# Two-bank score tiles for the first two batches of an attention and mixer kernel

## The chip, the cores and the metric

The kernel runs on one core of one Trainium2 chip. The time is that of the device for one launch, in microseconds, and the median of several runs is compared. A core has four engines that compute, each with an instruction queue of its own that runs in order: TensorE (PE, with its weight loads shown as PEld), VectorE (DVE), ScalarE (ACT) and GpSimd (POOL). SyncE (SP) starts transfers, as ACT and POOL do beside their other work. Matmul results go to PSUM, which has 8 banks of 512 fp32 columns on each of 128 partitions; everything else lies in SBUF.

## The reference

Eight batches of causal attention with 8 heads over 576 tokens, with a bias from a running sum of `s`, and behind it a mixer: a low-rank product over tokens and a two-layer perceptron with residuals.

```python
# attention: q, k, v (8, 8, 576, 64), s (8, 8, 576)
scores = scale * np.matmul(q, k.transpose(0, 1, 3, 2))
cum = np.cumsum(np.maximum(s, 0.0), axis=-1)
bias = -(cum[:, :, :, None] - cum[:, :, None, :])
scores = np.where(causal, -1000000000.0, scores + np.minimum(bias, 0.0))
attn = softmax(scores); out = np.matmul(attn, v)
# mixer: x (8, 576, 512) is out with its heads side by side
u = x + ((x.transpose(0, 2, 1) @ U) @ V).transpose(0, 2, 1)
return u + np.maximum(u @ w_ch1, 0.0) @ w_ch2
```

## The kernel before

Batches go in four pairs. While the perceptron of one pair runs on TensorE (`layer1`, `layer2`), the attention of the next pair runs between its matmuls. `beside` deals the two streams out by costs that each `yield` names, so the order of every engine's queue is fixed when the program is built. The first pair has nothing to run beside: batch 0's attention (`first_attention`) runs alone, and batch 1's (`second`) beside the first layer on batch 0's tokens.

A head's transposed scores are taken only where the causal mask leaves something. `scores` computes them in four steps, three of 448 columns and one of 256, each in a PSUM bank of its own from a ring of three (`bank("s", 3)`), each followed by one exponential on ScalarE (L329) into a row `p` of SBUF whose columns are named O0 to O3 (blocks off the diagonal) and D0 to D4 (diagonal blocks). GpSimd sets the diagonal blocks' other half to zero (L344). `weigh` multiplies by the values with 15 matmuls of 65 columns (L373) into a `pv` bank; the 65th column holds ones and gives the row sums, whose reciprocal (L379) VectorE multiplies in (L385).

The bias is added inside the score matmul: q and k have extra rows with the running sums, made by `cumulate` (scans L232, a small prefix matmul L236) and moved there by transfers (`direct_rows`, L261). q and k arrive by `load_six` with tokens on partitions, are transposed on TensorE (`turn_six`, L296, six matmuls into one bank), and two copies (L288) bring each result to its place. In batch 0 all eight heads keep their `p` until values have arrived (`fetch_v`, then `cast_v` on GpSimd, L200), so `weigh` for its first heads comes late (`weighed`). `fill` matmuls on zeros stand ahead of some score steps. `mix_first` makes the mixer's input for batch 0 once all its heads are weighed; then the first layer begins (L551).

In batch 1 `second_scores` computes all scores first, with transpositions between them (`turns`), and `second` weighs all heads behind that. From batch 2 on, `attention` weighs a head one behind its scores, q and k come through `cast` (a transfer that GpSimd issues, to bf16 rows in device memory, L155) and transposing transfers, and `at_head` says what is issued behind a head: the cast of batch 4 behind head 6 of batch 2, for one.

PSUM has three rings of banks: `f` with 3 (first and second layer, mixer, some transpositions), `s` with 3 (scores) and `pv` with 2 (weighing, transpositions).

## Time and profile before

| what | us |
|---|---|
| median of 3 runs (373.66 to 374.18) | 373.73 |
| the profiled execution, whole | 374.12 |
| its span, first to last instruction | 372.4 |

Busy time of the engines in the profiled execution, by stage:

| stage | us | PE | DVE | ACT | POOL |
|---|---|---|---|---|---|
| start, to the first scores | 0 to 9.05 | 6.82 | 7.33 | 5.54 | 7.54 |
| batch 0's attention, mixer input | 9.05 to 28.8 | 17.85 | 16.48 | 16.92 | 16.54 |
| batch 1 beside the first layer | 28.8 to 59.6 | 30.00 | 21.60 | 26.21 | 23.28 |
| second layer, transpositions for batch 2 | 59.6 to 79.2 | 19.24 | 13.12 | 6.81 | 4.61 |
| batches 2 and 3 | 79.2 to 123.9 | 43.62 | 14.93 | 37.65 | 19.13 |
| mixer input of the second pair, and the third and fourth pairs' work | 123.9 to 306.9 | 180.86 | 58.62 | 95.52 | 37.15 |
| the last pair's perceptron | 306.9 to 372.4 | 62.11 | 7.02 | 23.59 | 0 |

Matmuls overlap each other in the pipeline and their ends are modelled, so that a stage in which PE is called busy throughout may hold small waits; the distance between starts says more. A wait for several things is put down to the one that the profile shows last. In a timeline line the first number is the start in us from the span's start, the second the time that the run of instructions covers, then engine, source line, operation, output and input tile with shapes, and the count; idle time ahead of it and what ended it stand in square brackets.

### The profile page before, as it was taken

Reading aid. Unit: us, or ns where it says so; the run is one execution under the profiler, and the core shown is the slowest. Engines: PE = TensorE matmul, PEld = TensorE weight load, DVE = VectorE, ACT = ScalarE, POOL = GpSimd, SP = SyncE. Lnnn points to the kernel's source line nnn. Section 1 sums busy time; section 2 is a strip of 40 time slices with the busy share of each in tenths; the row PEclk is TensorE's granted clock in tenths of the full one; section 3 lists DMA queues with packets and bytes.
Section 4 is the critical chain, followed back from the end, with each engine's and each line's share of the span. In section 5 each row is a group of like instructions: output and inputs, shape, how many; then the busy total and the mean of one; then the engine's idle time right before and its main releaser. Section 6 shows DMA issues by size and latency. Waiting matters only on the chain.

```text
span 372.4 us, 8251 instructions
## 1 busy us (share of the span) xinstructions
PE 360.5 (97%) x3234; PEld 221.4 (59%) x3255; DVE 139.1 (37%) x310; ACT 212.3 (57%) x499; POOL 108.3 (29%) x166
## 2 busy tenths in 40 slices
PE   7899999999999989999999999999999999999996
PEld 3577684568776446666654446666654446565444
DVE  8878855652224551221243721212233710000221
ACT  6988982479897019889850009888840007772000
POOL 8895982312634103243150003242120000000000
PEclk9999999999999999999999999999999999999999
DMA  7999999798799869999995558892001550000122
GB/s 118 181 153 213 173 207 214 153 204 164 138 242 178 104 157 172 180 212 163 217 155 165 101 141 154 156 193 47 2 30 58 126 143 28 2 0 30 70 72 85
DMA packets 124039, 49.32 MB, mean 132 GB/s; under 512 B 104896, under 2 KB 119200, under 8 KB 124000
## 3 DMA queue, kind: packets, MB, share of 16 engines
q1 hardware_dynamic: 104374, 34.45, 45.6%
q0 software_dynamic: 19056, 14.22, 27.7%
q8 instruction: 25, 0.41, 0.5%
q10 hardware_dynamic: 570, 0.12, 0.2%
q14 instruction: 14, 0.11, 0.1%
HBM read 37.67 MB, written 15.79 MB: 144 GB/s over the span
## 4 chain that ended last, share of the span: by engine, by line
PE 87%; DVE 6%; ACT 3%; issue 1%; POOL 1%; DMA 1%; ACTq 0%; POOLq 0%; DVEq 0%
PE ps_f L551 32%; PE ps_f L570 31%; PE ps_s L323 11%; PE ps_pv L373 8%; DVE x_sb L522 2%; ACT pT L329 1%; PE ps_f L518 1%; PE ps_f L444 1%; PE ps_pv L296 1%; DVE qT L288 1%; DVE kT L288 1%; PE ps_s L315 1%; ACT x_sb L329 1%; DMA uT<-x_sb 1%; ACT hT L558 1%
## 5 line engine op out<-in xcount | busy, mean ns | idle before, releaser
L551 PE MATMUL ps_f<-uT,w 128*128 128x384 bf16 (+3 forms) x832 | 158.4, 313 | 0.9 <-DMA uT<-x_sb 0.9
L329 ACT ACTIVATE pT<-ps_s 128x448 bf16<-128x448 f32 x232 | 109.8, 526 | 60.4 <-PE ps_s L323 58.6
L570 PE MATMUL ps_f<-w,hT 128*128 128x512 bf16 (+1 forms) x571 | 136.8, 373 | 1.1
L558 ACT ACTIVATE hT<-ps_f 128x384 bf16<-128x384 f32 (+3 forms) x208 | 101.9, 492 | 46.8 <-PE ps_f L551 45.5
L551 PEld LDWEIGHTS <-w 128*128 128x128 bf16 x832 | 72.3, 98 | 34.0 <-issue 2.2
L570 PEld LDWEIGHTS <-hT 128*128 128x128 bf16 x592 | 54.9, 98 | 57.1 <-issue 3.9
L344 POOL TENSOR_SCALAR_AFFINE_SELECT pT<-pT 128x640 bf16<-128x640 bf16 x58 | 43.9, 756 | 150.5 <-ACT pT L329 150.0
L323 PE MATMUL ps_s<-qT,kT 68*128 68x128 bf16 (+9 forms) x576 | 80.8, 239 | 3.2 <-ACT pT L329 0.8
L323 PEld LDWEIGHTS <-kT 68*128 68x128 bf16 (+1 forms) x576 | 46.2, 97 | 29.9 <-issue 5.5
L379 DVE RECIPROCAL rec<-ps_pv 128x5 f32<-128x5 f32 x64 | 12.5, 195 | 120.2 <-PE ps_pv L373 119.9
L581 DVE TENSOR_TENSOR o<-x_sb,ps_f 128x512 f32<-128x512 bf16 (+1 forms) x37 | 24.9, 673 | 86.3 <-PE ps_f L570 85.6
L373 PEld LDWEIGHTS <-pT 128*128 128x128 bf16 x870 | 33.7, 97 | 8.7 <-ACT pT L329 1.0
L373 PE MATMUL ps_pv<-v_raw,pT 128*128 128x65 bf16 x870 | 36.7, 194 | 0.7 <-POOL pT L344 0.5
L385 DVE TENSOR_TENSOR x_sb<-ps_pv,rec 128x320 bf16<-128x320 f32 (+1 forms) x64 | 29.3, 458 | 2.3
L200 POOL CAST v_raw<-vf 128x512 bf16<-128x512 f32 (+1 forms) x35 | 21.3, 616 | 16.3 <-DMA vf<-in_v_dram 11.4
L522 DVE TENSOR_TENSOR x_sb<-x_sb,ps_f 128x512 bf16<-128x512 bf16 x32 | 21.2, 687 | 7.4 <-PE ps_f L518 7.1
L288 DVE COPY kT<-ps_pv 64x576 bf16<-64x576 bf16 x14 | 11.2, 803 | 3.5 <-ACT kT L288 2.8
L296 PEld LDWEIGHTS <-hT 96*128 96x128 bf16 x144 | 8.1, 97 | 4.4 <-DMA hT<-in_k_dram 1.1
L518 PE MATMUL ps_f<-ux_sb,V_cat 128*128 128x512 bf16 x27 | 10.2, 379 | 0.4
L288 DVE COPY qT<-ps_pv 64x576 bf16<-64x576 bf16 x12 | 9.6, 803 | 2.5 <-ACT qT L288 1.8
L315 PE MATMUL ps_s<-uT 128*128 128x512 bf16 (+2 forms) x21 | 7.6, 451 | 1.8 <-DVE uT L106 1.6
L288 ACT COPY kT<-ps_pv 64x576 bf16<-64x576 bf16 x4 | 3.2, 796 | 9.2 <-PE ps_pv L296 9.2
(109 smaller groups left out, 152.0 us busy)
## 6 DMA issues: line engine op xcount, KB each, us to landing
out_dram<-o SPq DMA_DIRECT2D x31, 256.0 KB
vf<-in_v_dram SPq DMA_DIRECT2D x28, 256.0 KB
w<-in_moe_w_ch_dram POOLq DMA_DIRECT2D x8, 512.0 KB, 9.4
kq_rows<-in_k_dram POOLq DMA_DIRECT2D x5, 576.0 KB, 7.0
kq_rows<-in_q_dram POOLq DMA_DIRECT2D x5, 576.0 KB, 10.0
out_dram<-o SPq DMA_DIRECT2D x10, 128.0 KB
hT<-in_k_dram POOLq DMA_DIRECT2D x4, 288.0 KB, 8.6
hT<-in_q_dram POOLq DMA_DIRECT2D x4, 288.0 KB, 10.6
```

What stands on the lines that cost most here:

```text
L200: (engine or nc.gpsimd).tensor_copy(v_raw[b // 2 % 2][n, 5 * (b % 2) + t, :, :D], vf0[n, t])
L288: one()
L323: nc.tensor.matmul(ps[:, col : col + w], lhsT=kt_[:rows, c + kc : c + kc + 128], rhs=qt_[:rows, c + qc : c + qc + w], start=True, stop=True,)
L329: nc.scalar.activation(p[:, at : at + w], ps[:, :w], EXP, scale=scale)
L344: nc.gpsimd.affine_select(out=diagonal, in_=diagonal, compare_op=ALU.is_ge, fill=0.0, base=0, pattern=[[0, 5], [1, 128]], channel_multipli ...
L373: nc.tensor.matmul(pv3[:, it, :], lhsT=p[:, at : at + 128], rhs=vr[:, 5 * bi + j, h, :], start=(j == 0), stop=(j == it),)
L385: nc.vector.tensor_mul(x[:, 5 * bi : 5 * bi + n, h * D : h * D + D], pv3[:, :n, :D], rec[:, :n].unsqueeze(2).to_broadcast([128, n, D]),)
L522: nc.vector.tensor_add(x[:, t, :], x[:, t, :], hp_)
L551: nc.tensor.matmul(f1[:, :cw], lhsT=w1[:, kt, 128 * nf : 128 * nf + 128], rhs=uT[:, kt, c0:c1], start=(kt == 0), stop=(kt == 3),)
L558: nc.scalar.activation(hT[:, nf, c0:c1], f1[:, :cw], RELU)
L570: nc.tensor.matmul(f2[:, :cw], lhsT=hT[:, kt, 128 * t : 128 * t + 128], rhs=w2[:, kt, cs], start=(kt == 0), stop=(kt == 15 and not more),)
L581: nc.vector.tensor_add(o[:, :cw], x_sb[g % 2][:, t, cs], f2[:, :cw])
```

## The change

- For the first two batches, `scores` puts two banks into one tile (`wide`, 2 tiles of 1024 columns). A head has two exponentials in place of four: one over 2 x 448 columns in two banks (a strided pattern), one over 704 columns. The first head of batch 0 keeps its first two halves apart (`together` false), 448, 448 and 704. The order of the score steps changes (second with its diagonal, then last with its diagonal, then first with the rest), and the layout of `p` with it (O3 before O2, and 64 columns more in a row).
- PSUM is dealt twice. At first there are 3 `f` banks, 2 `wide` tiles of two banks and 1 `pv` bank. When batch 1's scores are all issued, `deal` gives the `wide` and `pv` banks back and makes 3 `s` and 2 `pv` banks out of them. From batch 2 on scores are computed as before.
- In batch 0: q's first transposition goes to an `f` bank; V_cat's first half is copied later, by VectorE and GpSimd in place of ScalarE and GpSimd (`place_V` behind the last transposition); the last transposition has one of its copies on ScalarE; two clearings of the value tile go from VectorE to GpSimd; transpositions come at other steps; the value casts are spread as (4, 0), 1, 2, 3 behind heads 1 to 4; k's load for batch 1 is issued ahead of the cast behind head 3; five `weigh`s in place of six stand between the scores, and they alternate between `pv` and `f` banks.
- In batch 1 the second transposition comes one step later.
- The cast of batch 4 (the fifth batch) is issued behind head 4 of batch 2 in place of head 6.

In the diff, the places where only `bank("f", 3)` becomes `bank("f")` are left out.

```diff
-O0, O2, O3, O1, D3, PAD, D4, D0, D1, D2, P_W = (
-    0, 448, 640, 704, 1024, 1152, 1216, 1280, 1408, 1536, 1664)
+O0, O3, O2, O1, D3, PAD, D4, D0, D1, D2, P_W = (
+    0, 448, 512, 704, 1024, 1152, 1216, 1280, 1408, 1536, 1728)
 AUG = 4
...
     work = ctx.enter_context(tc.tile_pool(name="work", bufs=2))
-    psum = ctx.enter_context(tc.tile_pool(name="psum", bufs=2, space=bass.MemoryType.PSUM))
-    def bank(tag, bufs):
-        return psum.tile([128, 512], FP32, tag=tag, bufs=bufs, name="ps_" + tag)
+    psum = ctx.enter_context(tc.tile_pool(name="psum", bufs=3, space=bass.MemoryType.PSUM))
+    early, late = ExitStack(), ExitStack()
+    ctx.enter_context(late)
+    PSUM = bass.MemoryType.PSUM
+    pools = {"f": (psum, 3, 512)}
+    pool = early.enter_context(tc.tile_pool(name="early", bufs=2, space=PSUM))
+    pools.update(wide=(pool, 2, 1024), pv=(pool, 1, 512))
+    def deal():
+        early.close()
+        pool = late.enter_context(tc.tile_pool(name="late", bufs=2, space=PSUM))
+        pools.update(s=(pool, 3, 512), pv=(pool, 2, 512))
+    def bank(tag):
+        pool, bufs, columns = pools[tag]
+        return pool.tile([128, columns], FP32, tag=tag, bufs=bufs, name="ps_" + tag)
...
-        pb = bank(tag, 2 if tag == "pv" else 3).bitcast(BF16)
+        pb = bank(tag).bitcast(BF16)
         for hh in range(2):
...
-    def scores(n, hh, p, fills=0):
+    def scores(n, hh, p, fills=0, together=None):
         kt_, qt_, c = kT[n % RING], qT[n % RING], hh * S
...
-        ps = bank("s", 3)
+        def last_and_diagonal(ps):
+            one(ps, 0, S - 128, 512, 64)
+            for j in range(3):
+                one(ps, 64 + 128 * j, 128 * j, 128 * j, 128)
+        def second_and_diagonal(ps):
+            one(ps, 0, 128, 256, 320)
+            one(ps, 320, 384, 384, 128)
+        def mask():
+            diagonal = p[:, D3 : D3 + 640].rearrange("p (t c) -> p t c", c=128)
+            nc.gpsimd.affine_select(
+                out=diagonal, in_=diagonal, compare_op=ALU.is_ge, fill=0.0, base=0,
+                pattern=[[0, 5], [1, 128]], channel_multiplier=-1,
+            )
+        if together is None:
+            ps = bank("s")
+            last_and_diagonal(ps)
+            exp(ps, D4, 448)
+            yield 0.2
+            ps = bank("s")
+            second_and_diagonal(ps)
+            exp(ps, O1, 448)
+            mask()
+            yield 0.19
+            ps = bank("s")
+            one(ps, 0, 0, 128, 448)
+            exp(ps, O0, 448)
+            yield 0.19
+            ps = bank("s")
+            one(ps, 0, 384, 512, 64)
+            one(ps, 64, 256, 384, 192)
+            exp(ps, O3, 256)
+            yield 0.11
+            return
+        ps = bank("wide")
         if fills:
             fill(ps, fills)
-        one(ps, 0, S - 128, 512, 64)
-        for j in range(3):
-            one(ps, 64 + 128 * j, 128 * j, 128 * j, 128)
-        exp(ps, D4, 448)
+        second_and_diagonal(ps)
+        if not together:
+            exp(ps, O1, 448)
+        yield 0.19
+        last_and_diagonal(ps[:, 512:])
+        if together:
+            two = lambda t: t.rearrange("p (i c) -> p i c", c=512)[:, :, :448]
+            nc.scalar.activation(two(p[:, O1 : O1 + 1024]), two(ps), EXP, scale=scale)
+        else:
+            exp(ps[:, 512:], D4, 448)
+        mask()
         yield 0.2
-        ps = bank("s", 3)
-        one(ps, 0, 128, 256, 320)
-        one(ps, 320, 384, 384, 128)
-        exp(ps, O1, 448)
-        diagonal = p[:, D3 : D3 + 640].rearrange("p (t c) -> p t c", c=128)
-        nc.gpsimd.affine_select(
-            out=diagonal, in_=diagonal, compare_op=ALU.is_ge, fill=0.0, base=0,
-            pattern=[[0, 5], [1, 128]], channel_multiplier=-1,
-        )
-        yield 0.19
-        ps = bank("s", 3)
+        ps = bank("wide")
         if fills:
...
         one(ps, 0, 0, 128, 448)
-        exp(ps, O0, 448)
-        yield 0.19
-        ps = bank("s", 3)
-        one(ps, 0, 256, 384, 192)
-        one(ps, 192, 384, 512, 64)
-        exp(ps, O2, 256)
-        yield 0.11
-    def weigh(b, h, p, scalar=False):
+        one(ps, 448, 384, 512, 64)
+        yield 0.22
+        one(ps, 512, 256, 384, 192)
+        exp(ps, O0, 704)
+        yield 0.09
+    def weigh(b, h, p, scalar=False, tag="pv"):
         bi = b % 2
...
         off = (O0, O1, O2, O3)
-        pv = bank("pv", 2)
+        pv = bank(tag)
         pv3 = pv[:, : 5 * (D + 1)].rearrange("p (t e) -> p t e", e=D + 1)
...
         turns = {
-            (0, 1): (1, 0), (0, 3): (1, 1), (1, 3): (2, 0), (2, 2): (2, 1), (3, 3): (3, 0), (4, 2): (3, 1)
+            (0, 1): (1, 0), (1, 0): (1, 1), (1, 3): (2, 0), (2, 2): (2, 1), (3, 3): (3, 0), (4, 2): (3, 1)
         }
...
             p = next_p()
-            for n, cost in enumerate(scores(HP + h // 2, h % 2, p)):
+            for n, cost in enumerate(scores(HP + h // 2, h % 2, p, together=True)):
                 yield cost
...
         load_six(0, i, 6, 8)
-    ps = bank("s", 3)
+    nc.gpsimd.memset(v_raw[0][:, :, :, D : D + 1], 1.0)
+    nc.gpsimd.memset(v_raw[0][:64, TAIL], 0.0)
+    ps = bank("wide")
     for _ in range(6):
...
         turn_six(0, 0, 0)
-        turn_six(0, 0, 1, scalar=2)
+        turn_six(0, 0, 1, scalar=2, tag="f")
         place_U(0, nc.scalar.copy)
-        place_V(0, (nc.scalar.copy, nc.gpsimd.tensor_copy))
-        ps = bank("s", 3)
+        ps = bank("wide")
         for _ in range(3):
...
             nc.vector.memset(p[:, PAD:D4], 1.0)
-        nc.vector.memset(v_raw[0][:, :, :, D : D + 1], 1.0)
-        nc.vector.memset(v_raw[0][:64, TAIL], 0.0)
         clear(zeros, 0.0)
...
         turns = {
-            (2, 0): (2, 0, "f"), (2, 3): (2, 1, "pv"), (3, 2): (3, 0, "pv"), (4, 1): (3, 1, "f")
+            (1, 3): (2, 0, "f"), (2, 3): (2, 1, "pv"), (3, 3): (3, 0, "f"), (4, 1): (3, 1, "f")
         }
-        weighed = {(5, 1): 1, (5, 3): 1, (6, 1): 1, (6, 3): 1, (7, 1): 1, (7, 3): 1}
+        weighed = {(5, 3): 1, (6, 1): 1, (6, 3): 1, (7, 1): 1, (7, 3): 1}
         halves = [mix_first(dt) for dt in (0, 2)]
         done = []
+        places = iter(["pv", "f"] * HP)
         for h in range(H):
...
             fills = 0 if h < 2 or h > HP else 320 if h < HP else 448
-            for n, _ in enumerate(scores(h // 2, h % 2, p, fills=fills)):
+            for n, _ in enumerate(scores(h // 2, h % 2, p, fills=fills, together=h > 0)):
                 if (h, n) in turns:
                     hp, which, tag = turns[h, n]
-                    turn_six(0, hp, which, tag=tag)
+                    turn_six(0, hp, which, tag=tag, scalar=hp == HP - 1 and which)
+                    if hp == HP - 1 and which == 1:
+                        place_V(0, (nc.vector.tensor_copy, nc.gpsimd.tensor_copy))
                 for _ in range(weighed.get((h, n), 0)):
-                    weigh(*done.pop(0))
+                    weigh(*done.pop(0), tag=next(places))
             done.append((0, h, p))
-            for t in {1: (4, 0), 2: (1, 2), 3: (3,)}.get(h, ()):
+            if h == 3:
+                load_six(1, 0, 0, HP)
+            for t in {1: (4, 0), 2: (1,), 3: (2,), 4: (3,)}.get(h, ()):
                 cast_v(0, t)
-            if h in (3, 4):
-                load_six(1, h - 3, 0, HP)
+            if h == 4:
+                load_six(1, 1, 0, HP)
             if h == 5:
...
         next(one)
-        weigh(*done.pop(0))
+        for _ in range(2):
+            weigh(*done.pop(0), tag=next(places))
         next(one)
         next(one)
-        weigh(*done.pop(0))
+        weigh(*done.pop(0), tag=next(places))
...
         k_copies = turned(
-            1, 0, 0, "s", [(heads[0], on_scalar), (heads[1], on_vector)]
+            1, 0, 0, "wide", [(heads[0], on_scalar), (heads[1], on_vector)]
         )
...
             pass
-        q_copies = turned(1, 0, 1, "s", [(hs, on_vector) for hs in heads])
+        q_copies = turned(1, 0, 1, "wide", [(hs, on_vector) for hs in heads])
         for copy in q_copies[:2] + k_copies[2:] + q_copies[2:]:
...
         yield from second_front
+        deal()
         for head in second_done:
...
                 turn_batch(c + 1)
-            if h == 6 and c == 2:
+            if h == 4 and c == 2:
                 cast(c + 2)
```

## The prediction

> **What bounds the kernel now.** I read the page first, then the timelines of each engine over the two places that the diff touches (9 to 60 us and 90 to 102 us). The page says that TensorE sets the time:
>
> ```profile
> span 372.4 us, 8251 instructions
> PE 360.5 (97%) x3234; PEld 221.4 (59%) x3255; DVE 139.1 (37%) x310; ACT 212.3 (57%) x499; POOL 108.3 (29%) x166
> ```
>
> So a change is worth what it moves PE. Counting each matmul at its unhindered step, PE stands still for 3.5 us between 9 and 18.4 us, for 2.5 us between 28.8 and 47.6, for 1 us or less per 20 us behind that. PE's marks:
>
> ```profile
> 18.36 0.62 PE L373 MATMUL ps_pv<-v_raw,pT 128*128 128x65 bf16 x15
> ...
> 24.67 0.63 PE L373 MATMUL ps_pv<-v_raw,v_raw 128*128 128x65 bf16 x15
> ...
> 28.80 1.58 PE L551 MATMUL ps_f<-uT,w 128*128 128x256 bf16 x12
> ...
> 31.03 0.35 PE L323 MATMUL ps_s<-qT,kT 68*128 68x320 bf16 x2 [0.23 <-DVE kT L764]
> ...
> 45.65 0.29 PE L236 MATMUL ps_f<-v_raw,before 72*72 72x6 f32 x2
> ...
> 47.62 0.62 PE L373 MATMUL ps_pv<-v_raw,pT 128*128 128x65 bf16 x15
> ...
> 99.88 0.64 PE L373 MATMUL ps_pv<-v_raw,pT 128*128 128x65 bf16 x15 [0.49 <-POOL pT L344]
> ```
>
> These are the first batch's first and last `weigh`, the first layer's start, the second batch's scores held by a copy, the prefix matmul, its first `weigh`, and a `weigh` held by GpSimd. ScalarE's timeline:
>
> ```profile
> 9.59 6.45 ACT L329 ACTIVATE pT<-ps_s 128x448 bf16<-128x448 f32 x16
> 16.70 1.69 ACT L329 ACTIVATE pT<-ps_s 128x448 bf16<-128x448 f32 x4 [0.66 <-PE ps_s L323]
> ...
> 48.21 0.79 ACT L329 ACTIVATE v_raw<-ps_s 128x256 bf16<-128x256 f32 x1
> ```
>
> Sixteen exponentials run without a gap, so ACT bounds the first heads; the second batch's last one ends at 49.00, 1.38 us after PE has begun to weigh. VectorE and GpSimd:
>
> ```profile
> 32.01 1.62 DVE L288 COPY kT<-ps_pv 64x576 bf16<-64x576 bf16 x2
> 33.67 1.61 DVE L288 COPY qT<-ps_pv 64x576 bf16<-64x576 bf16 x2
> ...
> 43.36 2.24 DVE L232 TENSOR_TENSOR_SCAN v_raw<-sel 72x64 f32<-72x64 f32 x6
> ```
>
> ```profile
> 10.62 0.66 POOL L146 CAST V_cat<-w 32x576 bf16<-32x576 f32 x1
> ...
> 17.96 0.61 POOL L200 CAST v_raw<-vf 128x512 bf16<-128x512 f32 x1
> ...
> 55.56 0.46 POOL L806 MEMSET v_raw<- 128x80 bf16 x1 [1.15 <-ACT x_sb L390]
> 56.08 0.99 POOL L808 MEMSET v_raw<- 64x520 bf16 x2
> ...
> 97.22 0.74 POOL L155 DMA_DIRECT2D kq_rows<-in_q_dram  x1
> 97.95 1.18 POOL L200 CAST v_raw<-vf 128x512 bf16<-128x512 f32 x2
> 99.08 0.75 POOL L344 TENSOR_SCALAR_AFFINE_SELECT pT<-pT 128x640 bf16<-128x640 bf16 x1
> ```
>
> Copies follow each other without a gap because two `pv` banks alternate, and the six scans lie behind the last copy.
>
> **Prices.** Starts of queued exponentials lie 0.424 us apart at 448 columns and 0.264 at 256: 0.83 ns a column and 0.051 an instruction. So 2x448 takes 0.80, 704 takes 0.64, and a head 1.44 instead of 1.54. The trace has no exponential over two banks; at worst it pays the fixed part per bank (0.85), at best this is right. I take 0.80. A result is free about 0.11 us after its step, PE follows 0.05 later, and ACT starts about 0.2 after PE's last issue (0.165 until the matmul ends, 0.04 to the next engine). PE's steps: 0.055 for 128 columns, 0.19 for 448, 0.25 for six transposes, 0.45 for a `weigh`. DVE's copy of half a head pair: 0.81.
>
> **First batch.** Removed: V_cat's copy from ACT (0.6, of which 0.14 shows, as PE's first scores stand at 9.05 behind the rows that ACT's queue issued until 7.07), and 0.4 us of clearing from DVE (which waits for transposes behind it). The scores now need two banks before ACT may start, and there are two such tiles where three single ones rotated. Walked head by head: the first exponential starts at 9.45; the built program makes the second half of head 0 wait for the first half's exponential, so the second starts at 10.45. From there each 2x448 waits for its tile: 0.11 + 0.05 until free, fill matmul 0.14, six score matmuls 0.39, 0.2 to ACT is 0.89, against 0.64 of other exponential: 0.25 lost per head, 0.10 won. Head 3 is done at 16.47 (16.04 before). The transposes one quantum earlier put the copies for heads 4 and 5 at 15.8 (16.25 before), and head 4 at 16.78 (16.70). Then ACT takes one of the last four copies (0.81), so head 4 is done at 19.03, head 5 at 20.47.
> POOL decides the first `weigh`, which needs the fourth V cast. From 10.57: two clearings 0.96 (rows L806, L808), masks 0.70 each, casts 0.6, a load's issue 0.67, V_cat 0.66: two clearings, two masks, two casts, mask, cast, mask, load, cast, mask, V_cat, cast, with head 3's exponential waited for until 16.0, gives 19.9 (before 17.96 + 0.61 = 18.57). Behind this cast wait the load of q, head 5's mask and w1's first load, all earlier than or within 0.3 us of before. PE, queued behind its wait, has three more `weigh`s to do behind the last scores than ACT's pace hides: 0.45 each, alternating `weigh` 0.45 and scores 0.3 to 0.4 from 19.95, plus 0.2 for division of head 3 before the token sums (0.20 + 0.49 on DVE). The last `weigh` starts at 25.53, not 24.67: **+0.86**. If the cast were there in time, -0.3; with the extra fixed part, +1.2.
>
> **Second batch.** Four things, on the clock of before from 28.80. (1) The first score tile now reuses the bank of batch 1's k transposes, whose last copy ends at 30.98: PE stands from 30.22 to 31.03, with 0.42 more behind it than before (a score quantum and two L551). (2) Until the second batch's scores are over there is one `pv` bank. A transposition waits for the copies of the one before: 1.62 + 0.05 + 0.46 (six transposes to their end) + 0.04 is 2.17 per turn, not 1.63. Walking PE, ACT and DVE, PE waits 0.6, 0.4 and 0.3 at the second, third and fourth turn, 0.3 at the sixth, and the last copies end at 44.86, not 42.95. (3) The scans behind them end at 47.6 (45.6 before), and the prefix matmul holds PE for 0.66 until 47.65; behind it is the last head. (4) The banks are dealt anew there, and the built program's first `weigh` waits for the batch's last exponential, on which PE had 1.38 us lead. From 47.65: 0.15, a quantum 0.19, L551 and scores 1.3 to the last score matmul, ACT's queue (2x448, a relu 0.32, 704) until 50.55. First `weigh` at 50.6. Before it stood at 47.62 with 0.22 less of the first layer done: **+2.75**. ACT's gain of 0.1 per head is in the walk, and goes into idle time. From below, +1.3: point (4) alone, without a queue on ACT. From above +3.2.
> The trace has ACT busy for 26.2 of these 30.8 us, full from 35 to 45 and with gaps around. The Trainium skill (Perfetto Trace Analysis, Optimizing Scalar/DVE Operations) speaks against the change for the second case: where Scalar isn't saturated but makes bubbles on other engines, breaking its instructions up may let work finish sooner; where it is saturated, grouping helps. By the second half alone this part would be a gain of 8 times 0.10, 0.8; by the first it is a loss, as walked. It is why the faster rival below has no more than its 0.10.
>
> **Fifth cast.** Its two issues (0.72 each) stand between head 6's mask and head 7's, which therefore ends at 99.83. Moved to head 4, they fill an idle 1.96 us of POOL ahead of head 5's mask. The `weigh` at 99.88 could then start at 99.12, but its second matmul needs ACT's 448 columns (98.94 + 0.54) and its ninth the last 256 (99.75): done at 100.01 instead of 100.36, **-0.35** (0 to -0.65). The DMA share is 0.75 there and no PE wait names these rows.
>
> **Sum.** +0.86 + 2.75 - 0.35 = +3.26. Behind 60 us PE never waits for a due time, so a shift reaches the end. The profiled execution has 374.12 us, 372.4 of it span: 377.4, span 375.7. It lies 0.39 over the median 373.73, on which the same sum gives **377.0**.
>
> **Rivals.**
> *The waits cost less (0.15).* Turns and scans overlap better than walked, the first batch breaks even: +1.3 - 0.35 + 0.3, about 375.0. For it: PE's step counts have errors of 0.1 at each wait. Against: the turns' 2.17 is made of rows alone.
> *Faster: ACT is the bound, and what it saves arrives (0.10).* 31 instructions fewer, 0.051 each, is 1.57 us, plus 0.35: 371.8. It decides if the two-bank ring and the single `pv` bank hide behind exponentials, that is, if ACT stays gapless from 32 to 48 us and the first `weigh` of batch 2 starts at 47.6 or sooner. For it: ACT is gapless in the first 16 exponentials and full from 35 to 45 us. Against: PE is blocked at the second turn while ACT has nothing queued.
> The same section of the Trainium skill (Perfetto Trace Analysis, Optimizing Scalar/DVE Operations) puts a Scalar instruction's overhead on PSUM at about 51 ns, and the rows agree (0.051 us).
> *The halves cancel (0.03).* ACT's 1.57 and the cast's 0.35 pay for half of the second batch: 373.7, within 0.2%.
> *The change doesn't do what it says (0.02).* If a two-bank exponential pays its fixed part per bank, 31 times 0.051, 1.6 us of ACT's time, come on top; with some 1 us of it on the path, 378.
>
> **How the numbers follow.** My forecast has 0.70, with 375.8 to 378.1 as its own range. 0.2% (0.75 us) is about what a measurement of this kernel tells from no change. Slower 0.70 + 0.15 + 0.02 = 0.87, same 0.03, faster 0.10. The range takes in the low-cost rival and leaves out the faster one and the cancelling one: 374.4 to 378.1.
>
> **What would show it.** In the first batch: `weigh` starts at 19.5 to 20 on PE, held by POOL's cast; a gap of 0.2 before each 2x448. In the second: 0.8 us of PE idle before the first score tile, copies on DVE in pairs 0.5 us apart, the prefix matmul 2 us later, and more than 1 us of idle PE before its first `weigh`, released by ACT. In the third: the last mask of batch 2 within 0.1 us of its exponential, no POOL wait near 100. I am wrong if PE meets the second turn with the bank already free, or if the first layer starts before 28.8.

## The result and the profile after

The changed kernel takes 378.83 us (median of 5 runs, 377.51 to 379.15), the kernel before 373.73: 1.0122 times as long, 95% interval 1.0103 to 1.0141. Forecast was 377.0, in a range of 374.4 to 378.1: the sign was right, the size was not. The profiled execution took 379.15 us, 5.03 more than the one before.

The head of the page of the changed kernel; first its span, then busy time, share of the span and instructions by engine:

```profile
span 377.4 us, 8203 instructions
PE 360.5 (96%) x3234; PEld 221.5 (59%) x3255; DVE 138.2 (37%) x308; ACT 211.3 (56%) x468; POOL 109.2 (29%) x168
```

ScalarE has 31 instructions fewer and 1.0 us less to do. TensorE has the same 360.5 us of work in a span 5.0 longer: what was added is waiting (the granted clock was 1.00 in this execution). TensorE's timeline answers to the marks shown of before. (In this kernel `weigh` is L420, the scores L337, the transpositions L310, the prefix matmul L250, the first layer L598.)

```profile
19.34 0.44 PE L420 MATMUL ps_pv<-v_raw,pT 128*128 128x65 bf16 x9
20.26 0.34 PE L420 MATMUL ps_pv<-v_raw,pT 128*128 128x65 bf16 x6 [0.48 <-POOL v_raw L214]
20.93 0.55 PE L337 MATMUL ps_wide<-qT,kT 128*128 128x320 bf16 x6 [0.33 <-DVE rec L426]
...
26.30 0.62 PE L420 MATMUL ps_f<-v_raw,v_raw 128*128 128x65 bf16 x15
...
30.50 1.58 PE L598 MATMUL ps_f<-uT,w 128*128 128x256 bf16 x12
32.70 0.35 PE L337 MATMUL ps_wide<-qT,kT 68*128 68x320 bf16 x2 [0.62 <-DVE kT L816]
...
35.68 0.43 PE L310 MATMUL ps_pv<-identity,hT 96*128 96x96 bf16 x6 [0.46 <-DVE kT L302]
...
37.91 0.41 PE L310 MATMUL ps_pv<-identity,hT 96*128 96x96 bf16 x6 [0.31 <-DVE qT L302]
...
49.26 0.29 PE L250 MATMUL ps_f<-v_raw,before 72*72 72x6 f32 x2
...
52.52 0.61 PE L420 MATMUL ps_pv<-v_raw,pT 128*128 128x65 bf16 x15 [1.11 <-ACT v_raw L343]
...
142.22 0.48 PE L598 MATMUL ps_f<-uT,w 128*128 128x384 bf16 x2 [1.92 <-DMA uT<-x_sb]
```

The first `weigh` is cut in two by GpSimd's cast; the last one stands at 26.30 (24.67 before), the first layer at 30.50 (28.80). In the second batch the first scores wait for the copies of batch 1's k, the transpositions for VectorE's copies, and the first `weigh` for the batch's last exponential: it starts at 52.52 (47.62). The last line is one that the forecast had nothing for: the second pair's first layer waits 1.92 us for `uT`, which transfers transpose out of `x`. In the profile of before the same wait is 0.89:

```profile
137.19 0.48 PE L551 MATMUL ps_f<-uT,w 128*128 128x384 bf16 x2 [0.89 <-DMA uT<-x_sb]
```

VectorE's copies and ScalarE's exponentials show the same:

```profile
33.99 1.64 DVE L302 COPY kT<-ps_pv 64x576 bf16<-64x576 bf16 x2 [0.33 <-PE ps_pv L310]
36.15 1.61 DVE L302 COPY qT<-ps_pv 64x576 bf16<-64x576 bf16 x2 [0.52 <-PE ps_pv L310]
38.36 1.62 DVE L302 COPY kT<-ps_pv 64x576 bf16<-64x576 bf16 x2 [0.60 <-PE ps_pv L310]
...
47.28 1.93 DVE L246 TENSOR_TENSOR_SCAN v_raw<-sel 72x64 f32<-72x64 f32 x6
```

```profile
11.65 0.92 ACT L393 ACTIVATE pT<-ps_wide 128x896 bf16<-128x896 f32 x1
12.47 0.75 ACT L343 ACTIVATE pT<-ps_wide 128x704 bf16<-128x704 f32 x1
...
50.54 0.95 ACT L393 ACTIVATE v_raw<-ps_wide 128x896 bf16<-128x896 f32 x1
51.34 0.48 ACT L605 ACTIVATE hT<-ps_f 128x320 bf16<-128x320 f32 x1
51.65 0.81 ACT L343 ACTIVATE v_raw<-ps_wide 128x704 bf16<-128x704 f32 x1
```

Copies come in pairs half a us apart where they were gapless, and the scans end at 49.2 instead of 45.6. The exponential over two banks starts 0.82 us before the next: the forecast's 0.80.

The span falls into three parts that can be compared between all runs: from the first scores to the first layer (first batch), from there to the third batch's first `weigh` (second batch and first layer), and the rest. The first two are distances between two starts on TensorE, the third goes on to the end of the span; all three are from the one profiled execution of each kernel. The median is that of the runs compared, and each ratio is to the runs of the kernel before beside them; the last column counts those among them with a mean granted clock under 0.997. Runs more than 1.5% above the fastest of their kernel are left out (one each of weigh_before_deal, turns_and_weigh and three_repairs, two of first_as_before_repaired_second). The kernels are told of in the next section.

| kernel | first batch | second batch | rest | median us | ratio to before, 95% | clock under 0.997 |
|---|---|---|---|---|---|---|
| before | 19.75 | 52.48 | 291.10 | 373.73 | 1 | 1 of 67 beside the others |
| changed | 21.41 | 55.10 | 291.83 | 378.83 | 1.0122 (1.0103, 1.0141) | 2 of 5 |
| changed_again | 22.29 | 55.09 | 289.76 | 379.31 | 1.0141 (1.0124, 1.0158) | 3 of 4 |
| first_batch_alone | 23.40 | 52.53 | 289.91 | 376.68 | 1.0063 (1.0042, 1.0084) | 5 of 6 |
| second_batch_alone | 19.64 | 55.08 | 289.77 | 375.71 | 1.0047 (1.0030, 1.0063) | 0 of 8 |
| cast_alone | 20.19 | 52.02 | 290.03 | 373.48 | 1.0002 (0.9979, 1.0024) | 1 of 12 |
| after_cast_late | 20.95 | 55.10 | 290.06 | 377.63 | 1.0114 (1.0093, 1.0135) | 2 of 6 |
| weigh_before_deal | 20.95 | 53.80 | 289.75 | 376.12 | 1.0065 (1.0046, 1.0083) | 0 of 5 |
| turns_two_banks | 20.96 | 53.51 | 289.75 | 376.28 | 1.0080 (1.0056, 1.0104) | 1 of 6 |
| turns_and_weigh | 23.71 | 52.38 | 289.82 | 375.89 | 1.0054 (1.0035, 1.0074) | 5 of 11 |
| first_as_before_repaired_second | 19.62 | 52.43 | 290.03 | 373.99 | 1.0015 (0.9992, 1.0038) | 1 of 10 |
| v_cast_sooner | 20.32 | 55.08 | 289.75 | 377.50 | 1.0087 (1.0061, 1.0113) | 1 of 6 |
| casts_then_load | 20.75 | 54.67 | 289.76 | 376.78 | 1.0069 (1.0053, 1.0085) | 0 of 6 |
| weigh_sooner | 19.74 | 55.08 | 289.79 | 376.90 | 1.0084 (1.0071, 1.0097) | 0 of 6 |
| fills_in_pauses | 22.10 | 52.53 | 289.93 | 375.36 | 1.0029 (1.0008, 1.0049) | 0 of 7 |
| changed_with_fills | 22.11 | 55.12 | 289.76 | 377.92 | 1.0110 (1.0097, 1.0123) | 0 of 4 |
| three_repairs | 21.75 | 51.59 | 290.73 | 375.86 | 1.0052 (1.0032, 1.0071) | 0 of 5 |
| all_repairs | 20.02 | 52.35 | 291.52 | 375.33 | 1.0040 (1.0021, 1.0059) | 2 of 8 |

Single profiles of the same stage differ, and the border between the first two columns is loose: cast_alone, with the first batch of the kernel before, waits 0.42 for the first layer's weights and so has 20.19 instead of 19.75, and its second batch, which then has no wait for the copies of batch 1's k, is 0.46 shorter. In the profiled execution the first batch costs 1.66, the second 2.62, the rest 0.73; 0.05 more passes ahead of the first scores.

### The profile page after: what moved, and what is told of

The parts are those of the page before. It is cut to its first block, busy times and chain, and to the rows that moved or that the text cites. A ratio compares the mean times of both kernels' runs of the same rounds, so it can differ in the third digit from the quotient of the medians.

```text
span 377.4 us, 8203 instructions
## 1 busy us (share of the span) xinstructions
PE 360.5 (96%) x3234; PEld 221.5 (59%) x3255; DVE 138.2 (37%) x308; ACT 211.3 (56%) x468; POOL 109.2 (29%) x168
## 4 chain that ended last, share of the span: by engine, by line
PE 84%; POOL 5%; DVE 4%; ACT 2%; DMA 2%; issue 2%; SPq 0%; POOLq 0%; ACTq 0%; DVEq 0%
PE ps_f L598 30%; PE ps_f L617 30%; PE ps_s L337 9%; PE ps_pv L420 7%; DVE x_sb L569 2%; POOL pT L356 2%; PE ps_f L565 1%; POOL v_raw L201 1%; PE ps_f L491 1%; DMA hT<-in_k_dram 1%; ACT pT L343 1%; PE ps_wide L337 1%; POOL v_raw L214 1%; DMA uT<-x_sb 1%; PE ps_pv L310 1%
## 5 line engine op out<-in xcount | busy, mean ns | idle before, releaser
L598 PE MATMUL ps_f<-uT,w 128*128 128x384 bf16 (+3 forms) x832 | 158.3, 313 | 1.9 <-DMA uT<-x_sb 1.9
L605 ACT ACTIVATE hT<-ps_f 128x384 bf16<-128x384 f32 (+3 forms) x208 | 99.1, 479 | 47.0 <-PE ps_f L598 45.4
L343 ACT ACTIVATE pT<-ps_s 128x448 bf16<-128x448 f32 x192 | 91.4, 519 | 60.6 <-PE ps_s L337 58.5
L598 PEld LDWEIGHTS <-w 128*128 128x128 bf16 x832 | 73.3, 98 | 34.7 <-issue 3.2
L337 PEld LDWEIGHTS <-kT 68*128 68x128 bf16 (+1 forms) x576 | 46.3, 97 | 30.7 <-issue 5.7
L337 PE MATMUL ps_s<-qT,kT 68*128 68x128 bf16 (+4 forms) x432 | 61.4, 239 | 0.4 <-ACT pT L343 0.2
L426 DVE RECIPROCAL rec<-ps_pv 128x5 f32<-128x5 f32 x60 | 11.7, 195 | 122.2 <-PE ps_pv L420 122.1
L420 PEld LDWEIGHTS <-pT 128*128 128x128 bf16 x870 | 34.1, 97 | 9.9 <-issue 1.9
L420 PE MATMUL ps_pv<-v_raw,pT 128*128 128x65 bf16 x840 | 35.8, 194 | 1.9 <-ACT v_raw L343 1.1
L432 DVE TENSOR_TENSOR x_sb<-ps_pv,rec 128x256 bf16<-128x256 f32 (+1 forms) x60 | 27.4, 456 | 2.2
L337 PE MATMUL ps_wide<-qT,kT 128*128 128x320 bf16 (+5 forms) x144 | 18.0, 239 | 3.6 <-ACT pT L343 1.7
L310 PEld LDWEIGHTS <-hT 96*128 96x128 bf16 x144 | 8.1, 97 | 6.7 <-DMA hT<-in_k_dram 1.4
L302 DVE COPY kT<-ps_pv 64x576 bf16<-64x576 bf16 x12 | 9.6, 804 | 4.7 <-ACT kT L302 2.8
L329 PE MATMUL ps_wide<-uT 128*128 128x512 bf16 (+2 forms) x21 | 7.8, 464 | 2.2 <-DVE uT L120 1.6
```

The lines of the kernel that those rows point to most:

```text
L302: one()
L337: nc.tensor.matmul(ps[:, col : col + w], lhsT=kt_[:rows, c + kc : c + kc + 128], rhs=qt_[:rows, c + qc : c + qc + w], start=True, stop=True,)
L343: nc.scalar.activation(p[:, at : at + w], ps[:, :w], EXP, scale=scale)
L420: nc.tensor.matmul(pv3[:, it, :], lhsT=p[:, at : at + 128], rhs=vr[:, 5 * bi + j, h, :], start=(j == 0), stop=(j == it),)
L432: nc.vector.tensor_mul(x[:, 5 * bi : 5 * bi + n, h * D : h * D + D], pv3[:, :n, :D], rec[:, :n].unsqueeze(2).to_broadcast([128, n, D]),)
L598: nc.tensor.matmul(f1[:, :cw], lhsT=w1[:, kt, 128 * nf : 128 * nf + 128], rhs=uT[:, kt, c0:c1], start=(kt == 0), stop=(kt == 3),)
```

## The experiments

### The parts alone

**first_batch_alone** takes the second batch back to single banks and single exponentials:

```diff
-            for n, cost in enumerate(scores(HP + h // 2, h % 2, p, together=True)):
+            for n, cost in enumerate(scores(HP + h // 2, h % 2, p)):
...
+        deal()
         on_scalar, on_vector = [nc.scalar.copy] * 2, [nc.vector.tensor_copy] * 2
```

(with batch 1's first transpositions in `s` banks and its second turn behind quantum 3 again, and no dealing later).

> The changed kernel with the second batch as before: single banks, single exponentials, banks dealt anew ahead of it, turns as before. Theory (terms add: first batch +1.70, cast -0.3): first layer at 30.5, the stage behind it as long as before, 375.1 us. Rival (the late first layer is absorbed by the second batch, which had its own waits): 374.0 us or less.

**second_batch_alone** takes the first batch back (single banks, the old order of clearing, copies, casts and loads) and deals the banks to two-bank tiles behind it:

```diff
-            for n, _ in enumerate(scores(h // 2, h % 2, p, fills=fills, together=h > 0)):
+            for n, _ in enumerate(scores(h // 2, h % 2, p, fills=fills)):
...
+        deal_wide()
         on_scalar, on_vector = [nc.scalar.copy] * 2, [nc.vector.tensor_copy] * 2
```

> The changed kernel with the first batch as before (single banks, its copies and casts in the old order) and the banks dealt to two-bank tiles behind it. Theory (terms add: second batch +2.65, cast -0.3): first layer at 28.8 to 29.0, first weigh of the second batch at 50.8, 376.1 us. Rival (the second batch's loss hangs on the late first batch, whose loads and copies it meets): 374.8 us or less.

The second batch takes 55.08 with the edit and 52.53 without, whatever the first does, so it has a loss of its own of 2.6, as large as expected; second_batch_alone came out at 375.71, not under 374.8. The first batch's loss isn't absorbed either (the stage behind it takes 52.53, and 52.48 before), and it varies: 23.40 in the profile of first_batch_alone, 21.41 in the changed kernel. That difference was not expected; it is followed up under the first batch and the clock.

**cast_alone** is the kernel before with this edit, **after_cast_late** the changed kernel with its reverse:

```diff
-            if h == 6 and c == 2:
+            if h == 4 and c == 2:
```

> The kernel before with the fifth cast alone moved from head 6 to head 4. Theory (the cast gives more back on SyncE than it wins on GpSimd): PE's weigh near 100 us is 0.3 us sooner, but the cast's packets now lie beside the transposes of the fourth batch on SyncE's queue, which take 4 to 5 us instead of 1.4 to 2.3, the queue stays late up to the transposes of x, and PE's wait for uT near 137 us grows from 0.9 to about 1.9: net +0.7, 374.4 us. Rival (the later wait for uT comes from the 4 us by which the first stages are late, not from the cast): the 0.3 us arrives, 373.4 us, wait for uT at 0.9.

> The changed kernel with the fifth cast back at head 6. Theory (cast gives back on SyncE): PE loses 0.3 near 104 us and wins about 1.0 at the wait for uT near 142: 378.1 us. Rival (the wait comes from the shift of the first stages): 379.1 us, with a wait for uT of 1.6 or more.

My theory fell. Of cast_alone the median is 373.48 and TensorE stands 0.30 us at the place of the wait for `uT`, less than before rather than more, so the rival's 373.4 is what was seen (its wait of 0.9 is not), though the interval of the ratio (0.9979 to 1.0024) can't tell it from no change. after_cast_late has no wait for `uT` either, and its rest is 290.06, where eight kernels with the cast at head 4 have 289.75 to 289.79 (three more have 289.82 to 289.93, and cast_alone and first_as_before_repaired_second have 290.03 with 0.3 us of the `uT` wait in it). The timelines show the same worth more directly: from the third batch's first `weigh` to the one that follows the `weigh` held by GpSimd is 22.49 us in before and 22.48 in after_cast_late, 22.16 in cast_alone and 22.17 in the changed kernel. So the cast is worth 0.3.

The wait for `uT` comes and goes with the execution, in kernels with the cast early and late: 0.89 before, 1.92 in the changed kernel, none when the same code ran again (rest 289.76). SyncE's queue, which issues the transpositions of `x`, gives it in every profile. Before, changed and changed again:

```profile
131.93 6.53 SPq L526 DMA_TRANSPOSE uT<-x_sb  x5
```

```profile
136.96 6.53 SPq L573 DMA_TRANSPOSE uT<-x_sb  x5
```

```profile
135.18 6.53 SPq L573 DMA_TRANSPOSE uT<-x_sb  x5
```

In the seven profiles in which TensorE stands at this place (by 0.06 to 2.1 us), the layer starts 5.25 to 5.28 us behind that first issue (137.19 and 142.22 in the two waits shown). Where the queue is earlier, the layer starts when the ten matmuls ahead of it are done, 5.80 us behind the issue in changed_again and 6.41 to 6.93 in the other profiles. What makes the queue late is open.

### The second batch

**weigh_before_deal**:

```diff
         yield from second_front
-        deal()
-        for head in second_done:
-            weigh(*head)
+        for n, head in enumerate(second_done):
+            weigh(*head, tag=("pv", "wide")[n % 2])
             yield 0.48
+        deal()
```

> The changed kernel with the second batch's eight weighs ahead of the dealing of the banks, in the single pv bank and the two-bank tiles in turn. Theory (the new deal makes the first weigh wait for the last exponential): PE's 1.27 us ahead of the first weigh go, 377.6 us. Rival (PE would meet another wait there, for the masks or the copies, so that it is late anyway): 378.5 us or more.

**turns_two_banks**:

```diff
-                    turn_six(1, *turns[h, n])
+                    turn_six(1, *turns[h, n], tag=next(tags))
```

with `tags = iter(["pv", "f"] * HP)`.

> The changed kernel with the second batch's transpositions in the pv bank and an f bank in turn. Theory (the single pv bank makes each transposition wait for the copies of the one before): PE's waits of 0.63, 0.48, 0.36 and 0.28 ahead of transpositions go, and so does the 0.22 at the prefix matmul; VectorE's copies follow without a gap; part of it comes back where the two-bank ring waits for ScalarE and where the first layer waits for its f bank: 377.6 us (376.9 to 378.2). Rival (ScalarE bounds the stage): 378.5 us or more, the waits of PE now ahead of scores.

TensorE's timeline of weigh_before_deal where the 1.11 had been, and VectorE's of turns_two_banks:

```profile
51.01 0.38 PE L598 MATMUL ps_f<-uT,w 128*128 128x256 bf16 x2
51.23 0.62 PE L420 MATMUL ps_pv<-v_raw,pT 128*128 128x65 bf16 x15
51.69 0.65 PE L598 MATMUL ps_f<-uT,w 128*128 128x256 bf16 x4
52.18 0.62 PE L420 MATMUL ps_wide<-v_raw,pT 128*128 128x65 bf16 x15
```

```profile
34.16 1.62 DVE L302 COPY kT<-ps_pv 64x576 bf16<-64x576 bf16 x2 [0.33 <-PE ps_pv L310]
35.81 1.61 DVE L302 COPY qT<-ps_f 64x576 bf16<-64x576 bf16 x2
37.46 1.63 DVE L302 COPY kT<-ps_pv 64x576 bf16<-64x576 bf16 x2
39.33 1.62 DVE L302 COPY qT<-ps_f 64x576 bf16<-64x576 bf16 x2 [0.24 <-PE ps_f L310]
```

The first `weigh` follows the first layer's matmuls without a wait, and the stage is 1.30 shorter (55.10 to 53.80). With two banks the copies follow each other nearly gapless, 1.59 shorter (to 53.51). Both medians, 376.12 and 376.28, are lower than expected, as the changed kernel's 378.83 holds more than these waits.

**turns_and_weigh** has both edits; **first_as_before_repaired_second** adds them to second_batch_alone.

> The changed kernel with both changes of the second batch: transpositions in pv and f in turn, weighs ahead of the dealing. Theory (the two waits are separate terms, 1.29 and 1.43): the second layer's start moves 2.6 ahead of the changed kernel's (from 65.4 to about 62.8), 374.9 us where no wait for uT near 140 comes on top. Rival (both free the same time, the last exponentials bound it): 1.4 to 1.8 ahead, 375.9 us.

> The first batch as before, the second with two-bank tiles, transpositions in two banks and weighs ahead of the dealing; cast at head 4. Theory (repaired, the second batch costs nothing more than before, and ScalarE's 0.10 per head goes into idle time): 373.3 us, 0.4 under the kernel before, all of it the cast. Rival (ScalarE bounds the second batch once the banks don't): 372.8 us or less, with the second layer's start at 58.8 or earlier.

The terms nearly add (2.72 together, 1.30 and 1.59 alone): 52.38 and 52.43, against 52.48 before. These two waits are the whole loss of the second batch. And the stage isn't shorter than before although ScalarE does eight heads with 0.1 us less each: no rival in which ScalarE bounds it holds. The median of the second is 373.99 and not 373.3; its interval (0.9992 to 1.0038) includes no change. The median of turns_and_weigh, 375.89, is 1.0 above what was expected. Five of its 11 runs had a low clock, but from run to run its times don't follow the clock (375.13 at 0.995, 377.15 at 0.999), so that this 1.0 isn't explained.

### The first batch

**v_cast_sooner** has the first of these edits, **casts_then_load** both, which puts the load of k behind the casts:

```diff
-            for t in {1: (4, 0), 2: (1,), 3: (2,), 4: (3,)}.get(h, ()):
+            for t in {1: (4, 0), 2: (1,), 3: (2, 3)}.get(h, ()):
                 cast_v(0, t)
```

```diff
-            if h == 3:
-                load_six(1, 0, 0, HP)
...
-            if h == 4:
-                load_six(1, 1, 0, HP)
+            if h in (3, 4):
+                load_six(1, h - 3, 0, HP)
```

> The changed kernel with the first batch's fourth V cast right behind the third, ahead of head 4's mask and V_cat's copy on GpSimd. Theory (GpSimd's cast holds the first weigh, and with it the scores of head 6 queued behind it): no stop inside the first weigh, scores of head 6 at 20.2 instead of 20.9, first layer at 29.8 instead of 30.5: 376.8 us without a wait for uT near 140, 378.1 with one. Rival (the rows of heads 6 and 7, or the mask that is now later, hold PE at the same place): first layer at 30.3 or later.

> The changed kernel with GpSimd's order behind head 3 as it was before: third and fourth V cast, and only then the second batch's load of k. Theory (the late cast and the early load are what stops TensorE at 20 us: the cast holds the first weigh, the load's packets delay the rows of heads 6 and 7, and TensorE's pause there is what lets its granted clock fall to 0.5 for some 3 us in part of the runs): first layer at 29.4, all runs at a clock of 0.998 or more, 376.3 us median with a spread of about 1. Rival (the load and the clock have nothing to do with it): clocks of 0.995 in a third of the runs or more.

GpSimd's timeline of the changed kernel says what the first `weigh` waits for:

```profile
16.71 0.67 POOL L178 DMA_DIRECT2D hT<-in_k_dram  x1
17.38 0.63 POOL L214 CAST v_raw<-vf 128x512 bf16<-128x512 f32 x1
17.94 0.76 POOL L356 TENSOR_SCALAR_AFFINE_SELECT pT<-pT 128x640 bf16<-128x640 bf16 x1
18.76 0.66 POOL L160 CAST V_cat<-w 32x576 bf16<-32x576 f32 x1
19.48 0.72 POOL L214 CAST v_raw<-vf 128x512 bf16<-128x512 f32 x1
```

TensorE's timeline of v_cast_sooner, with that cast ahead of the mask:

```profile
19.09 0.46 PE L337 MATMUL ps_wide<-qT,kT 128*128 128x448 bf16 x3 [0.75 <-ACT pT L343]
19.39 0.62 PE L420 MATMUL ps_pv<-v_raw,pT 128*128 128x65 bf16 x15
...
25.26 0.62 PE L420 MATMUL ps_f<-v_raw,v_raw 128*128 128x65 bf16 x15
...
29.46 1.58 PE L598 MATMUL ps_f<-uT,w 128*128 128x256 bf16 x12
```

No cut in the `weigh`, and the stage takes 20.32 instead of 21.41. So the theory holds for the cast; but 0.57 of loss stays, where the forecast had a gain of 0.3 for this case. The median, 377.50, is 0.7 above what was expected, the profiled execution (376.05) 0.7 below. casts_then_load showed the clock held in all six runs, and no more: its first layer stood at 30.09 and not 29.4, as TensorE waits 0.40 us for the first layer's weights. GpSimd asks for them 0.5 later than in v_cast_sooner; that this is why they are late isn't shown, for cast_alone asks as early as the kernel before (21.38, 21.25) and waits 0.42. And since the clock fell in only one run of v_cast_sooner, the load's part in the rows' delay isn't shown.

**weigh_sooner** is v_cast_sooner with the first `weigh` back between head 5's scores:

```diff
-        weighed = {(5, 3): 1, (6, 1): 1, (6, 3): 1, (7, 1): 1, (7, 3): 1}
+        weighed = {(5, 1): 1, (5, 3): 1, (6, 1): 1, (6, 3): 1, (7, 1): 1, (7, 3): 1}
...
-        for _ in range(2):
-            weigh(*done.pop(0), tag=next(places))
+        weigh(*done.pop(0), tag=next(places))
```

> The changed kernel with the fourth V cast behind the third, and the first weigh back between head 5's scores, so that two and not three weighs follow the last head's scores. Theory (with the cast in time ScalarE is without a gap up to the end of head 7, as before, and what is left of the loss is one weigh of 0.45 more behind that end): first layer at 29.0 instead of 29.46, 376.3 us. Rival (the two-bank ring and the late first exponential make the rest, so that a weigh more or less behind it moves nothing): first layer at 29.3 or later.

The stage takes 19.74, against 19.75 before and 20.32 with the `weigh` behind. So the first batch's loss is made of three pieces: 0.58 for a `weigh` moved behind the last scores, 0.63 for the cast (20.32 to the 20.95 of three profiles), and 0.46 in the profiled execution of the changed kernel for scores of head 6 that came late (20.95 to 21.41). The first two are differences between single profiles, and all_repairs, with the first batch of weigh_sooner, has 20.02. The third varies most: behind the second part of the first `weigh` the scores of head 6 are late by nothing in those three profiles, by 0.44 in the changed kernel, 0.86 in first_batch_alone, 1.00 in changed_again and 1.16 in turns_and_weigh. The page names a reciprocal there in the changed kernel, but in weigh_before_deal these scores start ahead of it (20.94, 21.09). Where the wait is long it names the rows that transfers bring: `[1.05 <-DMA qT<-parts]` in turns_and_weigh, `[0.75 <-DMA kT<-parts]` in first_batch_alone. And with both edits undone the stage is as long as before and no shorter, though ScalarE saves 0.1 per head here too. The median, 376.90, is 0.6 above what was expected of it; the profiled execution, whose clock held and which had no wait for `uT`, took 375.80.

### The clock

In the profiles of first_batch_alone and turns_and_weigh the first batch takes 23.4 and 23.7. Views by window of TensorE alone: start and end in us, length, busy time (matmuls), granted clock, DMA share, GB/s. First turns_and_weigh:

```profile
18.40:21.80 3.40, 1.10 (x19) 1.00 0.71 99
22.50:25.50 3.00, 3.00 (x45) 0.50 1.10 156
26.00:27.00 1.00, 0.95 (x23) 1.00 1.23 204
```

then the kernel before:

```profile
18.40:21.80 3.40, 3.22 (x78) 1.00 0.56 73
22.50:25.50 3.00, 3.00 (x68) 1.00 1.26 185
26.00:27.00 1.00, 1.00 (x15) 1.00 1.28 194
```

TensorE is busy for 1.10 us out of 3.4 around 20 us, since the cast and the rows stop it; at 22.4 its granted clock falls to 0.50 and stays there until 25.85, so that 3 us hold 45 matmuls and not 68. To see whether the pause is the cause, fill matmuls, which add nothing to the result, were put into the two pauses.

```diff
+        for _ in range(fills):
+            fill(pv, 448)
         pv3 = pv[:, : 5 * (D + 1)].rearrange("p (t e) -> p t e", e=D + 1)
...
-                    weigh(*done.pop(0), tag=next(places))
+                    weigh(*done.pop(0), tag=next(places), fills=2 if h == 5 else 0)
...
+        for _ in range(more):
+            fill(ps, 448)
         second_and_diagonal(ps)
```

with `more=4` for head 6: **fills_in_pauses** is this on first_batch_alone, **changed_with_fills** on the changed kernel, **changed_again** the changed kernel beside it.

> The changed first batch with the second batch as before (the kernel in which five of six runs had a clock of 0.995), with fill matmuls put into the two pauses of TensorE near 20 us: two of 448 columns ahead of the first weigh, four ahead of head 6's scores. They add nothing to the result. Theory (the pause lets the clock fall): every run at 0.998 or more, 375.4 us median, although up to 0.5 us of fill comes on top. Rival (the clock falls for another reason, such as the work before): 0.995 in most runs, 376.7 us or more.

> The changed kernel once more, beside the three others. Theory (two kinds of run: 377.5 us where the clock holds, some 1.5 us more where it falls behind TensorE's pauses near 20 us): at least one run in four at 0.996 or less, these at 378.6 us or more, the others at 377.3 to 378.2. Rival (the clock has no part in it): no relation of time to clock.

> The changed kernel with fill matmuls in TensorE's two pauses near 20 us, two of 448 columns ahead of the first weigh and four ahead of head 6's scores; they add nothing to the result. Theory (the pause lets the clock fall): every run at 0.998 or more, 377.8 us median (0.3 for the fills). Rival (the clock falls for another reason): runs at 0.995 as often as without the fills, 379 us.

All 11 runs with fills have a clock of 0.998 or more; without them it is under 0.996 in 5 of 6 and 3 of 4, and in 18 of the 43 runs compared of all seven kernels with this first batch. So filling the two pauses keeps the clock up, and the thin work near 20 us is what lets it fall there. It is not the only occasion: the clock is low in 3 of 31 runs of the kernels with the cast in time, and in 3 of 97 with the first batch of the kernel before; where it fell in those, no trace shows. The medians are lower with the fills, 375.36 instead of 376.68 and 377.92 instead of 379.31, although the fills take TensorE's time. What a fall costs can be read between two marks on TensorE, the scores of head 6 and the first layer. In changed_again the clock held, in first_batch_alone it fell:

```profile
21.78 0.55 PE L337 MATMUL ps_wide<-qT,kT 128*128 128x320 bf16 x6 [0.89 <-DVE x_sb L432]
...
31.36 1.58 PE L598 MATMUL ps_f<-uT,w 128*128 128x256 bf16 x12
```

```profile
21.45 0.55 PE L337 MATMUL ps_wide<-qT,kT 128*128 128x320 bf16 x6 [0.75 <-DMA kT<-parts]
...
32.59 1.58 PE L598 MATMUL ps_f<-uT,w 128*128 128x256 bf16 x12
```

That is 9.58 us and 11.14; it is 9.57 in the changed kernel and in both kernels with fills, 11.13 in turns_and_weigh. So a fall costs 1.56 us here. Run by run, changed_again agrees: 377.95 at a clock of 0.999 and 379.27, 379.34 and 379.70 at 0.994. In first_batch_alone the one run at 1.000, 376.16, lies among those at 0.995 (375.40 to 377.30), so other things vary as much. The window of changed_with_fills:

```profile
18.40:21.80 3.40, 2.27 (x26) 1.00 0.69 96
22.50:25.50 3.00, 2.94 (x72) 1.00 1.08 154
```

### The sum of the repairs

**three_repairs** is casts_then_load with both edits of the second batch, **all_repairs** is weigh_sooner with them.

> The changed kernel with GpSimd's order as in the run before, the second batch's transpositions in two banks, and its weighs ahead of the dealing. Theory (terms add): 376.3 - 2.65 = 373.7 us. Rival (the two repairs of the second batch free one time only): 374.8 us.

> The kernel of the run before with both repairs of the second batch (transpositions in two banks, weighs ahead of the dealing). Theory (terms add: first layer +0.2, second batch 0, cast -0.3): 373.7 us, the time of the kernel before. Rival (the first layer's weights, asked for later than before, hold the earlier first layer as they did in three_repairs): 375 us or more, with a wait for w in front of the first layer. Second rival (the saved ScalarE time arrives once nothing else is in the way): 372.5 us or less.

Neither reached the kernel before. three_repairs loses 1.27 us to the first layer's weights, at the place where casts_then_load lost 0.40; its second batch, begun late, is shorter for that (51.59). It stands another 0.98 at the place of the `uT` wait. all_repairs has no wait for the weights, though GpSimd asks for them no earlier than in three_repairs (22.11, 22.02), so why they come late there is open. Its two batches take 72.37 us together (72.23 before); four of its eight runs lie at 374.2 to 375.2, two have a clock of 0.994 or 0.995, and the profiled one waits for `uT`:

```profile
138.42 0.48 PE L599 MATMUL ps_f<-uT,w 128*128 128x384 bf16 x2 [1.58 <-DMA uT<-x_sb]
```

No version beats the kernel before by more than its interval.

## Why the prediction was right in sign and too small

*The second batch, +2.75: right.* 2.62 was measured. Of the walk's waits at the transpositions, 0.6, 0.4, 0.3 and 0.3, the trace has 0.63, 0.48, 0.36 and 0.28 (starts of matmuls less their unhindered step). With the 1.70 by which the stage began later, the prefix matmul was forecast at 49.35 and the first `weigh` at 52.3; they stand at 49.26 and 52.52. The two repairs take 1.30 and 1.59 off and 2.72 together, and the stage is then at 52.38 (52.48 before): the two mechanisms are shown, and with them that the stage has no other loss.

*The fifth cast, -0.35: right.* -0.32 by the `weigh` behind it, and the `weigh` near 100 us has no wait for GpSimd any more.

*The price of an exponential: right, and worth nothing.* 0.82 and 0.64 were measured for 0.80 and 0.64. Yet with their waits repaired, both batches take what they took before (19.74 in weigh_sooner and 52.43 in first_as_before_repaired_second, 20.02 and 52.35 together in all_repairs), so the 0.1 per head doesn't arrive on TensorE. The faster rival is gone with it. By the rule that the forecast cited, the Trainium skill's (Perfetto Trace Analysis, Optimizing Scalar/DVE Operations), grouping can help where ScalarE is saturated. The trace agrees in so far as ScalarE was not: it was busy for 26.21 of 30.8 us of the second batch's stage before, and the larger exponentials won nothing there.

*The first batch, +0.86: this is the step that failed.* 1.66 in the profiled execution. Up to GpSimd's cast the walk was near: ScalarE ends heads 4 and 5 within 0.05 of the forecast. The cast itself was forecast to end at 19.9 and ends at 20.20, as GpSimd's rows from 16.71 on take 3.49 us where their prices make 3.23. Then come the scores of head 6, whose rows the forecast let arrive in time, 0.44 late. The last `weigh`, forecast at 25.53, stands at 26.30: these two make nearly all of the 0.77. How the term was put together was wrong as well. "If the cast were there in time, -0.3" puts 1.16 on the cast; v_cast_sooner, with the cast in time, has +0.57, and the cast is worth 0.63. There ScalarE ends head 7 when it did before (23.64, 23.69), and the `weigh` moved behind that end is 0.58 on top. The two errors have opposite signs and partly cancel, so that the term is only 0.34 short of the 1.20 that remains without the rows' delay: that is luck.

*"Behind 60 us PE never waits for a due time, so a shift reaches the end": wrong at one place.* The profile of before showed a wait of 0.89 for `uT` at 137 us, which I passed over as small. It is 1.92 in the changed kernel's profiled execution and nil in 11 of the 18 profiles. In that execution it accounts for 1.03 of the 1.77 by which 5.03 exceeds 3.26, the first batch for 0.80; the other terms cancel to within 0.06. It is set by when SyncE's queue issues the transpositions of `x`. Why that is late in some executions is open; neither the cast nor the late stages decide it, as the changed kernel has the wait in one execution and not in another.

*The granted clock: missing from the forecast.* I had TensorE's pause near 20 us, by place and releaser, and priced it as lost time alone; where the clock falls behind it, it costs 1.56 more. In 2 of the 5 runs shown the clock was 0.994 or 0.995, at 378.83 and 379.04, and with the 379.15 of the `uT` wait these make the median. The other two have 377.51 and 377.82 at 0.999 and 1.000, 0.5 to 0.8 over the forecast of 377.0. That this is the first batch's term alone isn't shown, as no trace of these two was kept. The median was missed by 1.8.

## What to carry to other kernels

A tile of two banks is paid in rotation: before merging instructions of one engine, count how many banks are left for everyone else, and which waits the smaller ring and a late re-dealing create, for in the second batch here these were the whole price, and the saved 0.1 us per head arrived nowhere. On a kernel bound by TensorE, look at each piece of TensorE work that is moved behind another engine's last result: the one `weigh` moved so here came on top in full. And price a pause of TensorE not only by its length: look whether the work around it is thin enough for the clock to fall, and compare the clocks of all runs, not only of the profiled one.

## What was not expected of the hardware

The granted clock fell to 0.50 without any pause longer than 1.05 us. In the profiles where it fell TensorE had been busy for 1.10 and 1.43 us of the 3.4 us from 18.4 to 21.8; in those where it held, for 3.22, 2.71, 2.40, 2.27, 1.95, and once for 1.30 (changed_again). It stayed at half for 3.4 us, from 22.44 to 25.85 and from 22.07 to 25.48, under full load. In the 3.41 us that end with the fall TensorE had been busy for 1.74 and 1.70. The Trainium skill (TensorE: Matmul & The Clock Gate, What's actually happening) has the clock follow the activity in a free-running window of about 3.4 us, with half speed as the low state. Half speed and the length agree with these rows, and a window that runs freely would let the same work fall on either side, as 1.30 and 1.43 did; no run here shows the window itself. The same page (Why this matters for your kernels) warns of pauses above some 3 us; here pauses of 0.74, 0.51 and 1.05 us (turns_and_weigh) in thin work were enough.
